# Expert stage of a fused attention and mixture-of-experts kernel: weight splits, PSUM banks, count loads and tile order rearranged

## The chip, the core and the metric

The kernel runs on one core of a Trainium2 chip. Five queues work side by side, each in its own order: PE (the matrix engine; its weight loads are listed as PEld), ACT (scalar engine), DVE (vector engine), POOL (GpSimd) and SP (which here only issues DMAs). They wait for each other through semaphores. The metric is the device time of one execution in microseconds (us); the median of several executions counts. The profile shows one execution, and its span is the time from the first to the last instruction.

## The reference

Attention with a block mask, a dense feed-forward layer, then a layer of eight experts of which each token takes one. The change touches only the experts:

```python
def _moe2_ref(x, w_gate, w1, w2, capacity):     # x [1152, 512], w1 [8, 512, 1024], w2 [8, 1024, 512]
    logits = x @ w_gate
    expert_idx = np.argmax(logits, axis=1)
    ...
    disp = np.zeros((E, capacity, D))           # capacity 288: slots of an expert
    ...                                         # token i goes to the next free slot of its expert
    h = np.maximum(np.einsum('ecd,edf->ecf', disp, w1), 0.0)
    y = np.einsum('ecf,efd->ecd', h, w2)
    ...
    out[i] = gate_w[i] * y[expert_idx[i], pos[i]]
```

## The kernel before

There are three parts: attention, the dense layer with the router at its end, and `part3`, the experts. Part 3 takes the time from about 330 us to the end. In it the order of every engine is the order in which the code is written.

Every fp32 product is made of three matmuls on a high and a low half of each operand: high by high, and the two mixed ones. So each weight tile must be split before it is used: ACT writes the high half (`xh`, line 1128), DVE the rest (`xl`, line 87). An expert has eight weight tiles of 512 KB, four of `w1` (raw tile `ra`) and four of `w2` (`rb`), loaded by SP into a ring of 12 raw buffers (`load_x`). While expert e is computed, the tiles of expert e+1 are split: the list `todo` holds a pair of functions for each tile (high, low), and `compute` runs a few of them between its own steps (`run(his, n)`, `run(los, n)`).

An expert has up to 288 slots, in tiles of 128, 128 and 32 slots (`j` = 0, 1, 2). A tile is computed only if the expert's count says that it holds tokens: each is an arm of a `tc.If` on a register. In the trace twelve tiles are computed: two for expert 0, one each for 1, 2 and 3, two for 4, three for 5, two for 6, none for 7. For a tile, `compute(e, j)` does on PE: two halves of `hx` (12 matmuls each, line 1207, ReLU into `hr` on ACT, line 1213), four transposes each (`hT`, line 1218) whose result ACT and DVE split into `gh` and `gl`, and 24 matmuls into `acc` (line 1228). ACT scales `acc` into `o` (line 1254) and POOL scatters `o` to the output (line 1255).

The slots of the next expert are loaded as `rows` (line 1169) and transposed on PE by `turn_slots` (`dT`, line 1177), then split into `dh` (ACT, line 1180) and `dl` (DVE). For j = 0 this is done inside the first tile (`turn_next`), for j = 1 and 2 after the tile's arm. The slots of expert 0 are made differently: part 2 gathers them by matmuls into four PSUM banks (`bank`, line 790), and `first_out` splits these into `dh` and `dl` (ACT line 802, DVE lines 800 and 87).

The counts lie in SBUF (`state["count"]`, ready at 326.0 us). `count_of(e)` loads one number into a register of PE, ACT, DVE and POOL (line 1265) and adds a check of its bounds.

PSUM has eight banks. Part 2 holds them in the order l1 (2), acc (3), m (2), lg (1); the `bank` tiles are the two of l1 and two of acc. Part 3 takes the banks over in the order in which its pools are opened.

Of the kernel before, what the change touches and what calls it, by code (L numbers as in the profile page):

```python
# [9 lines left out]
FP32 = mybir.dt.float32  # L10
# [7 lines left out]
PSUM = bass.MemoryType.PSUM  # L18
# [24 lines left out]
def attention_ffn_moe(  # L43
# [13 lines left out]
    nc = tc.nc  # L57
    B, H, S, D = q.shape
    NT, DM = out.shape
# [26 lines left out]
    def split_lo(eng, lo, x, hi):  # L86
        eng.tensor_tensor(out=lo, in0=x, in1=hi.bitcast(FP32), op=ALU.subtract)  # L87
# [4 lines left out]
    def load_w(pool, e, i):  # L92

        c = i // 2
        shape, src = [([128, 1, FE], w1[e, c * 128:(c + 1) * 128, :]), ([128, 2, DM], w2[e, c * 256:(c + 1) * 256, :])][i % 2]
        r = pool.tile(shape, FP32, tag="raw", name="r" + "ab"[i % 2])
        nc.sync.dma_start(out=r, in_=src.rearrange("(k p) f -> p k f", p=128))
        return r
# [601 lines left out]
    CT = (cap + 127) // 128  # L700
# [6 lines left out]
    state = {}  # L707
# [415 lines left out]
    def conv_x(e, i, r, part=0, parts=1):  # L1123

        n = FE // parts
        hi, lo, r = (x.rearrange("p k f -> p (k f)")[:, n * part:n * (part + 1)] for x in (*xw[e, i], r))
        return (
            lambda: nc.scalar.activation(out=hi, in_=r, func=ACTF.Copy),  # L1128
            lambda: split_lo(nc.vector, lo, r, hi),
        )  # L1130

    def part3():
        y_stack.close()
        p3 = ExitStack()
# [3 lines left out]
        hp = p3.enter_context(tc.tile_pool(name="hp", bufs=2, side="right"))  # L1138


        ps_acc = p3.enter_context(tc.tile_pool(name="ps_acc3", bufs=1, space=PSUM))
        ps_l1 = [p3.enter_context(tc.tile_pool(name=f"ps_l1{i}3", bufs=2, space=PSUM)) for i in range(2)]
        ps_m = p3.enter_context(tc.tile_pool(name="ps_m3", bufs=1, space=PSUM))
        ps_t = p3.enter_context(tc.tile_pool(name="ps_t3", bufs=2, space=PSUM))
        stiles = [(128 * i, min(128, CP - 128 * i)) for i in range(CT)]
        dT = state["dT"]
        views = bass_types.dram_disjoint_views(out, E * CT)
        NF = FE // 128
        rows, gate, xraw = {}, {}, {}
        engines = [mybir.EngineType.PE, mybir.EngineType.Activation, mybir.EngineType.DVE, mybir.EngineType.Pool]  # L1150


        COME = [0, 1, 2, 3, 4, 6, 5, 7]
        LATE = 2

        def load_x(e, half):

            xs = xraw.setdefault(e, {})
            for z in range(NX // 2 * half, NX // 2 * (half + 1)):
                xs[COME[z]] = load_w(raw_p if ((e - 1) * NX + z) % 12 < 4 else raw_q, e, COME[z])  # L1160

        def new_gate(e):
            gate[e] = dp.tile([128, CT, 2], FP32, tag="gt", name="gt")

        def load_rows(e):

            r = rows[e] = dp.tile([128, CT, YW], FP32, tag="rows", name="rows", bufs=1)
            for j, (s0, n) in enumerate(stiles):
                nc.sync.dma_start(out=r[0:n, j, :], in_=disp[e * CP + s0:e * CP + s0 + n, :])
            new_gate(e)  # L1170
# [14 lines left out]
        def passes(x, w):  # L1185
            return [(x[0], w[0]), (x[0], w[1]), (x[1], w[0])]

        def compute(e, j, side=(), turn_next=lambda: None):


            s0, n = stiles[j]
            h, hr, g = {}, {}, {}
            his, los = ([x[y] for x in side] for y in range(2))
            acc = ps_acc.tile([128, DM], FP32, tag="acc", name="acc")

            def run(fs, k):
                for f in fs[:k]:
                    f()
                del fs[:k]

            def l1(c, half):

                if half == 0:
                    h[c] = ps_l1[j > 0].tile([128, 512], FP32, tag="l1", name="hx")
                todo = [(x, y, kk) for x, y in ((0, 0), (0, 1), (1, 0)) for kk in range(KD)]
                for i, (x, y, kk) in list(enumerate(todo))[6 * half:6 * half + 6]:
                    nc.tensor.matmul(  # L1207
                        out=h[c][0:n], lhsT=dT[j][x][:, kk], rhs=xw[e, 2 * kk][y][:, 0, c * 512:(c + 1) * 512],
                        start=(i == 0), stop=(i == len(todo) - 1),
                    )  # L1210
                if half == 1:
                    hr[c] = hp.tile([128, 512], FP32, tag="hr", name="hr", bufs=3)
                    nc.scalar.activation(out=hr[c][0:n], in_=h[c][0:n], func=ACTF.Relu)

            def turn(c):
                ps = ps_m.tile([128, 4, 128], FP32, tag="m", name="hT")
                for i in range(4):
                    nc.tensor.transpose(  # L1218
                        out=ps[:, i, 0:n], in_=hr[c][0:n, i * 128:(i + 1) * 128], identity=ident[0:n, 0:n]
                    )  # L1220
                g[c] = gh, gl = [hp.tile([128, 4, 128], F32R, tag="g" + x, name="g" + x) for x in "hl"]
                nc.scalar.activation(out=gh[:, :, 0:n], in_=ps[:, :, 0:n], func=ACTF.Copy)
                split_lo(nc.vector, gl[:, :, 0:n], ps[:, :, 0:n], gh[:, :, 0:n])

            def l2(c, half):
                for f in range(4 * c + 2 * half, 4 * c + 2 * half + 2):
                    for i, (x, y) in enumerate(passes(g[c], xw[e, f // 2 * 2 + 1])):
                        nc.tensor.matmul(  # L1228
                            out=acc[0:n], lhsT=x[:, f % 4, 0:n], rhs=y[:, f % 2, :],
                            start=(f == 0 and i == 0), stop=(f == NF - 1 and i == 2),  # L1230
                        )

            run(his, 3)
            run(los, 3)
            l1(0, 0)
            l1(0, 1)
            run(his, 1)
            l1(1, 0)
            turn(0)
            run(his, 1)  # L1240
            run(los, 2)
            l1(1, 1)
            l2(0, 0)
            run(his, 1)
            turn(1)
            run(los, 1)
            l2(0, 1)
            run(his, NX)
            turn_next()
            run(los, NX)  # L1250
            l2(1, 0)
            l2(1, 1)
            y = hp.tile([128, DM], FP32, tag="hr", name="o", bufs=3)
            nc.scalar.mul(y[0:n], acc[0:n], gate[e][0:n, j, 0:1])  # L1254
            nc.gpsimd.indirect_dma_start(  # L1255
                out=views[e * CT + j],
                out_offset=bass.IndirectOffsetOnAxis(ap=gate[e][0:n, j, 1:2].bitcast(I32), axis=0),
                in_=y[0:n],
                in_offset=None,
                bounds_check=NT - 1,  # L1260
                oob_is_err=False,
            )

        def count_of(e):
            return nc.values_load(state["count"][0:1, e:e + 1], engines=engines, min_val=0, max_val=cap)  # L1265

        load_x(1, 0)
        load_x(1, 1)
        new_gate(0)
        for j, (s0, n) in enumerate(stiles):  # L1270
            nc.sync.dma_start(out=gate[0][0:n, j], in_=disp[s0:s0 + n, DM:DM + 2])
        count = {0: count_of(0)}
        for e in range(E):
            new = e + 1 < E
            todo = []
            if new:
                load_rows(e + 1)
                for i in COME:
                    new_x(e + 1, i, xraw[e + 1][i])
                todo = [conv_x(e + 1, i, xraw[e + 1][i]) for i in COME]  # L1280
            if e + 2 < E:
                load_x(e + 2, 0)

            def turn_next():
                if new:
                    turn_slots(e + 1, 0)

            with tc.If(count[e] > 0) as some:
                compute(e, 0, todo[:-LATE], turn_next)
            if new:  # L1290
                with some.Else():
                    for f in todo[:-LATE]:
                        f[0]()
                        f[1]()
                    turn_next()
            for f in todo[-LATE:]:
                f[0]()
                f[1]()
            if e + 2 < E:
                load_x(e + 2, 1)  # L1300
            for j in range(1, CT):
                with tc.If(count[e] > 128 * j):  # L1302
                    compute(e, j)
                if new:
                    turn_slots(e + 1, j)
            if new:
                count[e + 1] = count_of(e + 1)
        p3.close()

    every = {  # L1310
# [7 lines left out]
    with tc.manual_schedule(engines=every):  # L1318
        part3()
# [27 lines left out]
```

## Time and profile before

| what | value |
|---|---|
| median of 3 executions | 507.99 us (506.66 to 511.79) |
| profiled execution | 506.51 us, span 504.7 us |
| PE busy over the span | 479.9 us (95%) |
| DVE, ACT, POOL busy | 344.2, 311.9, 118.9 us |
| from first `hx` matmul to last `acc` matmul | 332.02 to 497.02 us |
| PE busy between 332 and 497 us | 157.29 us of 165 |

The busy time of PE counts matmuls that overlap in its pipeline, so a new matmul of 512 columns starts every 0.23 us though each is shown as 0.4 us. In a row of the timeline a bracket at the end tells how long the engine had been idle before it and what ended the wait; the inference of the releaser can name an engine that was long done.

### The profile page before, as it was taken

Reading aid. Unit: us, or ns where it says so; the run is one execution under the profiler, and the core shown is the slowest. Engines: PE = TensorE matmul, PEld = TensorE weight load, DVE = VectorE, ACT = ScalarE, POOL = GpSimd, SP = SyncE. Lnnn points to the kernel's source line nnn. Section 1 sums busy time; section 2 is a strip of 40 time slices with the busy share of each in tenths; the row PEclk is TensorE's granted clock in tenths of the full one; section 3 lists DMA queues with packets and bytes.
Section 4 is the critical chain, followed back from the end, with each engine's and each line's share of the span. In section 5 each row is a group of like instructions: output and inputs, shape, how many; then the busy total and the mean of one; then the engine's idle time right before and its main releaser. Section 6 shows DMA issues by size and latency. Waiting matters only on the chain. (4 is left out here: it accounts for less than half of the span.)

```text
span 504.7 us, 8722 instructions
## 1 busy us (share of the span) xinstructions
PE 479.9 (95%) x2842; PEld 400.2 (79%) x2842; DVE 344.2 (68%) x834; ACT 311.9 (62%) x701; POOL 118.9 (24%) x219
## 2 busy tenths in 40 slices
PE   6899999999999999999999999989998989999994
PEld 6778887789998899999998988768776768786683
DVE  6789898869987999964554466565467974551451
ACT  4789899957775765643554455365567784652641
POOL 6477878530000000000000102501122330101211
PEclk9999999999999999999999999789999999999998
DMA  8788674314998873520130034278379876370100
GB/s 194 162 224 213 156 191 103 114 44 126 234 238 280 259 235 111 166 85 0 56 112 2 22 125 147 89 272 318 111 299 358 310 283 246 114 290 21 54 22 24
DMA packets 61254, 80.86 MB, mean 160 GB/s; under 512 B 33170, under 2 KB 33170, under 8 KB 61200
## 3 DMA queue, kind: packets, MB, share of 16 engines
q1 hardware_dynamic: 58368, 75.18, 48.6%
q0 software_dynamic: 1632, 4.72, 2.5%
q8 instruction: 28, 0.46, 0.4%
q10 hardware_dynamic: 1200, 0.30, 0.3%
q14 instruction: 26, 0.21, 0.1%
HBM read 62.17 MB, written 12.41 MB: 148 GB/s over the span
## 5 line engine op out<-in xcount | busy, mean ns | idle before, releaser
L260 PE MATMUL acc<-wbh,gh 128*128 128x512 f32 x144 | 57.3, 398 | 0.0
L260 PE MATMUL acc<-wbh,gl 128*128 128x512 f32 x144 | 57.1, 397 | 0.0
L260 PE MATMUL acc<-wbl,gh 128*128 128x512 f32 x144 | 57.1, 397 | 0.0
L916 POOL DMA_INDIRECT disp<-y_all,slot x9 | 9.1, 1014 | 199.9 <-DVE e L245 177.2
L87 DVE TENSOR_TENSOR xl<-rb,xh 128x1024 fp32r<-128x1024 f32 (+1 forms) x36 | 38.9, 1101 | 22.2 <-ACT xh L1128 22.2
L485 POOL TENSOR_SCALAR prob<-prob,stat 128x576 f32<-128x576 f32 (+3 forms) x80 | 42.0, 537 | 26.6 <-DVE stat L479 17.9
L458 ACT ACTIVATE prob<-s,stat 128x288 f32<-128x288 f32 (+4 forms) x96 | 45.3, 480 | 1.5 <-POOL kk L339 0.8
L243 ACT ACTIVATE e<-h 128x384 f32<-128x384 f32 x48 | 23.2, 484 | 36.7 <-PE h L233 34.3
L186 DVE SCALAR_TENSOR_TENSOR cv_t<-r,cv_t 128x512 int32<-128x512 int32 x64 | 44.2, 691 | 0.3
L87 DVE TENSOR_TENSOR xl<-ra,xh 128x1024 fp32r<-128x1024 f32 (+1 forms) x36 | 39.3, 1102 | 7.0 <-ACT xh L1128 6.1
L233 PE MATMUL h<-xh,wah 128*128 128x384 f32 x192 | 42.2, 341 | 0.2 <-DVE e L245 0.2
L233 PE MATMUL h<-xl,wah 128*128 128x384 f32 x192 | 41.6, 337 | 0.0
L233 PE MATMUL h<-xh,wal 128*128 128x384 f32 x192 | 41.1, 336 | 0.0
L245 DVE SCALAR_TENSOR_TENSOR e<-e,h 128x384 f32<-128x384 f32 x48 | 26.4, 550 | 21.3 <-ACT e L244 21.1
L1228 PE MATMUL acc<-xh,gh 128*128 128x512 f32 (+1 forms) x96 | 39.3, 410 | 0.0
L445 DVE TENSOR_REDUCE stat<-s 128x1 f32<-128x288 f32 (+4 forms) x96 | 37.5, 422 | 1.4 <-PE s L423 1.1
L233 PEld LDWEIGHTS h<-xh,wah 128*128 128x128 f32 x192 | 34.3, 188 | 4.9 <-DVE e L245 0.9
L1228 PE MATMUL acc<-xh,gl 128*128 128x512 f32 (+1 forms) x96 | 38.0, 395 | 0.0
L1228 PE MATMUL acc<-xl,gh 128*128 128x512 f32 (+1 forms) x96 | 37.8, 394 | 0.0
L1255 POOL DMA_INDIRECT out<-o,gt x12 | 11.7, 972 | 110.7 <-ACTq L1302 33.1
L1128 ACT ACTIVATE xh<-ra 128x1024 fp32r<-128x1024 f32 (+1 forms) x36 | 34.3, 962 | 5.0 <-PE h L233 2.8
L249 ACT ACTIVATE gh<-e 128x384 fp32r<-128x384 f32 x48 | 25.1, 523 | 16.6 <-DVE e L245 16.0
(172 smaller groups left out, 1174.8 us busy)
## 6 DMA issues: line engine op xcount, KB each, us to landing
ra<-in_moe_w SPq DMA_DIRECT2D x32, 512.0 KB, 5.9
rb<-in_moe_w SPq DMA_DIRECT2D x32, 512.0 KB, 7.4
r<-in_moe_w_in SPq DMA_DIRECT2D x16, 512.0 KB, 6.8
r<-in_moe_w_out SPq DMA_DIRECT2D x16, 512.0 KB, 4.0
disp<-z SPq DMA_DIRECT2D x18, 257.0 KB, 7.0
rows<-disp SPq DMA_DIRECT2D x14, 257.0 KB, 4.9
out<-z SPq DMA_DIRECT2D x9, 256.0 KB, 3.9
kr<-in_k SPq DMA_DIRECT2D x16, 128.0 KB, 3.3
```

Source lines behind the costliest of these rows:

```text
L87: eng.tensor_tensor(out=lo, in0=x, in1=hi.bitcast(FP32), op=ALU.subtract)
L186: nc.vector.scalar_tensor_tensor(out=st["t"], in0=x(), scalar=scalar, in1=st["t"], op0=op, op1=ALU.bitwise_or)
L233: nc.tensor.matmul(out=h[:, f, :], lhsT=w[:, kk, (f0 + f) * 128:(f0 + f + 1) * 128], rhs=x[:, kk, t0:t0 + n], start=(i == 0), stop=(i == l ...
L243: nc.scalar.activation(out=e, in_=hf, func=ACTF.Relu, scale=-1.0)
L245: nc.vector.scalar_tensor_tensor(out=e, in0=e, scalar=-1.0, in1=hf, op0=ALU.add, op1=ALU.max)
L249: nc.scalar.activation(out=gh, in_=ef, func=ACTF.Copy)
L260: nc.tensor.matmul(out=acc[t], lhsT=x[:, f, t * 128:(t + 1) * 128], rhs=w[:, f0 + f, :], start=(first and f == 0 and i == 0), stop=(last a ...
L445: nc.vector.tensor_reduce(out=stat[n][0][0:nq, t + b:t + b + 1], in_=banks[n, part, b][0:nq, c0:c0 + w], axis=AX.X, op=ALU.max, negate=True,)
L458: nc.scalar.activation(out=prob[n, part][0:nq, c0 + k0:c0 + k0 + w], in_=banks[n, part, b][0:nq, c0:c0 + w], func=ACTF.Exp, bias=stat[n][0 ...
L485: nc.gpsimd.tensor_scalar(out=p, in0=p, scalar1=stat[n][2][0:nq, t:t + 1], scalar2=0.0, op0=ALU.mult, op1=ALU.add)
L1128: lambda: nc.scalar.activation(out=hi, in_=r, func=ACTF.Copy),
L1228: nc.tensor.matmul(out=acc[0:n], lhsT=x[:, f % 4, 0:n], rhs=y[:, f % 2, :], start=(f == 0 and i == 0), stop=(f == NF - 1 and i == 2),)
```

## The change

1. **Splits.** The first arm gets all eight high splits, and the low splits but the last two; before, the last two tiles (`LATE`) were split after the arm, high and low. Inside `compute`, two tiles instead of three are split before the first `hx`, and most of the rest after `turn_next`, that is behind `gh` and `dh`.
2. **PSUM.** The pools of part 3 are opened in another order, so that the first `hx` lies where part 2 had its pool m.
3. **Counts.** All eight counts are loaded by one instruction on each engine, ahead of the first expert, and the check of the bounds is gone.
4. **Order.** The arms of j = 1 and 2 follow each other; both `turn_slots` come after them.
5. **Buffers.** `hr` gets one buffer and `o` two of its own; before, they shared three.
6. **Loads.** The `rows` of expert 1 are asked for ahead of the second half of its weights.

```diff
+        ps_l1 = [None, p3.enter_context(tc.tile_pool(name="ps_l113", bufs=2, space=PSUM))]
+        ps_t = p3.enter_context(tc.tile_pool(name="ps_t3", bufs=2, space=PSUM))
+        ps_m = p3.enter_context(tc.tile_pool(name="ps_m3", bufs=1, space=PSUM))
+        ps_l1[0] = p3.enter_context(tc.tile_pool(name="ps_l103", bufs=2, space=PSUM))
         ps_acc = p3.enter_context(tc.tile_pool(name="ps_acc3", bufs=1, space=PSUM))
-        ps_l1 = [p3.enter_context(tc.tile_pool(name=f"ps_l1{i}3", bufs=2, space=PSUM)) for i in range(2)]
-        ps_m = p3.enter_context(tc.tile_pool(name="ps_m3", bufs=1, space=PSUM))
-        ps_t = p3.enter_context(tc.tile_pool(name="ps_t3", bufs=2, space=PSUM))
...
-                    hr[c] = hp.tile([128, 512], FP32, tag="hr", name="hr", bufs=3)
+                    hr[c] = hp.tile([128, 512], FP32, tag="hr", name="hr", bufs=1)
...
-            run(his, 3)
-            run(los, 3)
+            run(his, 2)
+            run(los, 2)
             l1(0, 0)
             l1(0, 1)
-            run(his, 1)
             l1(1, 0)
             turn(0)
             run(his, 1)
-            run(los, 2)
+            run(los, 1)
             l1(1, 1)
             l2(0, 0)
             run(his, 1)
             turn(1)
             run(los, 1)
             l2(0, 1)
+            turn_next()
             run(his, NX)
-            turn_next()
             run(los, NX)
...
-            y = hp.tile([128, DM], FP32, tag="hr", name="o", bufs=3)
+            y = hp.tile([128, DM], FP32, tag="o", name="o")
...
-        def count_of(e):
-            return nc.values_load(state["count"][0:1, e:e + 1], engines=engines, min_val=0, max_val=cap)
-
         load_x(1, 0)
+        load_rows(1)
         load_x(1, 1)
...
-        count = {0: count_of(0)}
+        _, count = nc.values_load_multi_w_load_instructions(
+            state["count"], engines=engines, min_val=0, max_val=cap,
+            skip_runtime_bounds_check_because="a sum of ones, and its minimum with cap",
+        )
...
-                todo = [conv_x(e + 1, i, xraw[e + 1][i]) for i in COME]
+                his, los = zip(*(conv_x(e + 1, i, xraw[e + 1][i]) for i in COME))
...
-                compute(e, 0, todo[:-LATE], turn_next)
+                compute(e, 0, (his, los[:-LATE]), turn_next)
...
-            for f in todo[-LATE:]:
-                f[0]()
-                f[1]()
+            for f in los[-LATE:]:
+                f()
...
-                if new:
+            if new:
+                for j in range(1, CT):
                     turn_slots(e + 1, j)
-            if new:
-                count[e + 1] = count_of(e + 1)
```

On PE, at the entrance to the experts: the last matmul of part 2, the load of the count, the branch, and the first `hx` of expert 0, with the queues that each waits for. Before:

```order
L790 MATMUL bank<-one,xl 128x288
L1265 TENSOR_LOAD count [waits DVE_49,Activation_49,Pool_49]
L1265 ISA x2
L1288 COMPARE_AND_BRANCH
L1207 MATMUL hx<-xh,dh_2041 128x512 [waits DVE_49,PE_49,Activation_49]
L1207 MATMUL hx<-xh,dh_2041 128x512 x3
L1207 MATMUL hx<-xl,dh_2041 128x512 x4
L1207 MATMUL hx<-xh,dl_2042 128x512 x4
```

And now:

```order
L790 MATMUL bank<-one,xl 128x288
L1271 TENSOR_LOAD count [waits DVE_49,Activation_49,Pool_49]
L1292 COMPARE_AND_BRANCH
L1209 MATMUL hx<-xh,dh_2041 128x512 [waits DVE_49,PE_49]
L1209 MATMUL hx<-xh,dh_2041 128x512 [waits Activation_49] x3
L1209 MATMUL hx<-xl,dh_2041 128x512 x4
L1209 MATMUL hx<-xh,dl_2042 128x512 [waits DVE_49]
```

The two instructions that check the bounds are gone, and one wait ahead of the first `hx` has become waits of single matmuls on the slices of `dh` and `dl` that they read.

On ACT, the first arm of an expert, from the branch at its head to `o`. Before:

```order
L1128 ACTIVATE xh<-ra 128x1024
L1128 ACTIVATE xh<-rb 128x1024
L1128 ACTIVATE xh<-ra 128x1024
L1213 ACTIVATE hr<-hx 128x512
L1128 ACTIVATE xh<-rb 128x1024
L1222 ACTIVATE gh<-hT 128x512
L1128 ACTIVATE xh<-ra 128x1024
L1213 ACTIVATE hr<-hx 128x512
L1128 ACTIVATE xh<-ra 128x1024
L1222 ACTIVATE gh<-hT 128x512
L1180 ACTIVATE dh_2041<-dT 128x512
L1254 ACTIVATE o<-acc,gt 128x512
```

And now:

```order
L1128 ACTIVATE xh<-ra 128x1024
L1128 ACTIVATE xh<-rb 128x1024
L1215 ACTIVATE hr<-hx 128x512
L1224 ACTIVATE gh<-hT 128x512
L1128 ACTIVATE xh<-ra 128x1024
L1215 ACTIVATE hr<-hx 128x512
L1128 ACTIVATE xh<-rb 128x1024
L1224 ACTIVATE gh<-hT 128x512
L1182 ACTIVATE dh_2041<-dT 128x512
L1128 ACTIVATE xh<-ra 128x1024 x2
L1128 ACTIVATE xh<-rb 128x1024 x2
L1255 ACTIVATE o<-acc,gt 128x512
```

Two `xh` instead of three stand ahead of the first `hr`, four stand between `dh` and `o` where none stood, and the two that followed the arm are among these.

On PE, the end of an expert: the end of the arm of j = 2, the transposes of the next expert's slots, and the branch into the next expert. Before:

```order
L1302 UNCONDITIONAL_BRANCH x2
L1177 MATMUL dT<-ident,rows 128x32 x4
L1265 TENSOR_LOAD count
L1265 ISA x2
L1288 COMPARE_AND_BRANCH
L1207 MATMUL hx<-xh,dh_2041 128x512 x4
```

And now:

```order
L1304 UNCONDITIONAL_BRANCH x2
L1179 MATMUL dT<-ident,rows 128x128 x4
L1179 MATMUL dT<-ident,rows 128x32 x4
L1292 COMPARE_AND_BRANCH
L1209 MATMUL hx<-xh,dh_2041 128x512 x4
```

The transposes for j = 1 have come down from between the two arms, and the load of the next count has gone from between the transposes and the branch.

## Rows read from the trace of the kernel before

**Rows 1.** Waits of PE from 300 to 505 us: total, times, longest.

```profile
PE hT L1218 <- ACT hr L1213: 2.9, 3, 1.1
PE dT L1177 <- PEq L1302: 2.7, 9, 0.3
PE hx L1207 <- DVE dl L87: 2.3, 1, 2.3
PE hx L1207 <- ACT xh L1128: 1.3, 3, 0.4
...
PE hx L1207 <- ACTq L1302: 0.5, 1, 0.5
```

**Rows 2.** Timeline of PE at the entrance: start, duration, line, idle before.

```profile
329.41 0.32 PE L790 MATMUL bank<-one,xl 128*128 128x288 f32 x1
332.02 1.34 PE L1207 MATMUL hx<-xh,dh 128*128 128x512 f32 x4 [2.29 <-DVE dl L87]
...
337.84 0.60 PE L1218 MATMUL hT<-ident,hr 128*128 128x128 f32 x4
```

**Rows 3.** Windows: length, PE, PEld, DVE, ACT, POOL busy; granted clock; DMA share, GB/s.

```profile
329.00:330.00 1.00, 0.73 (x4) 0.50 (x3) 0.64 (x3) 0.72 (x4) 0.00 (x0) 0.78 0.04 12
...
332.00:333.00 1.00, 0.98 (x4) 0.87 (x5) 0.00 (x0) 0.89 (x1) 0.00 (x0) 0.93 0.69 254
333.00:334.00 1.00, 1.00 (x3) 0.73 (x3) 0.74 (x1) 1.00 (x2) 0.00 (x0) 0.50 1.04 426
```

**Rows 4.** Timeline of ACT at the entrance.

```profile
329.41 1.58 ACT L802 ACTIVATE dh<-bank 128x128 fp32r<-128x128 f32 x6 [0.20 <-PE bank L790]
...
332.11 1.06 ACT L1128 ACTIVATE xh<-ra 128x1024 fp32r<-128x1024 f32 x1 [0.53 <-DVE dl L87]
```

**Rows 5.** Line 1265, the count: ns min/median/max, first and last start.

```profile
L1265 PEldq TENSOR_LOAD <-count x8: 297/302/492, 326.1 to 497.8; - x8
L1265 PEldq FUSED_REGOPS  x8: 146/146/160, 326.7 to 498.2; - x8
...
L1265 ACTq TENSOR_LOAD <-count x8: 274/278/477, 331.5 to 498.5; - x8
```

**Rows 6.** Timeline of PE, expert 1 and the start of expert 2.

```profile
360.02 1.19 PE L1207 MATMUL hx<-xh,dh 128*128 128x512 f32 x4 [0.52 <-ACT dh L1180]
...
364.29 0.60 PE L1218 MATMUL hT<-ident,hr 128*128 128x128 f32 x4
...
373.03 0.63 PE L1177 MATMUL dT<-ident,rows 128*128 128x128 f32 x4 [0.30 <-PEq L1302]
...
374.80 1.19 PE L1207 MATMUL hx<-xh,dh 128*128 128x512 f32 x4 [0.43 <-ACT xh L1128]
...
380.29 0.66 PE L1218 MATMUL hT<-ident,hr 128*128 128x128 f32 x4 [1.04 <-ACT hr L1213]
```

**Rows 7.** Timeline of ACT, same stretch.

```profile
369.98 0.60 ACT L1180 ACTIVATE dh<-dT 128x512 fp32r<-128x512 f32 x1 [1.23 <-PE dT L1177]
372.82 0.69 ACT L1254 ACTIVATE o<-acc,gt 128x512 f32<-128x512 f32 x1 [2.24 <-PEq L1302]
373.40 1.99 ACT L1128 ACTIVATE xh<-rb 128x1024 fp32r<-128x1024 f32 x2
...
376.79 1.07 ACT L1128 ACTIVATE xh<-ra 128x1024 fp32r<-128x1024 f32 x1 [0.17 <-issue]
...
379.65 0.58 ACT L1213 ACTIVATE hr<-hx 128x512 f32<-128x512 f32 x1
```

**Rows 8.** Line 1302 from 498.7 to 500 us: branches past empty expert 7.

```profile
L1302 PEldq COMPARE_BRANCH  x2: 218/322/427, 498.9 to 499.6; - x2
```

**Rows 9.** Timelines of SP's DMA issues and of POOL after the entrance.

```profile
333.93 1.88 SPq L1169 DMA_DIRECT2D rows<-disp  x3
...
341.01 1.09 POOL L1182 COPY gt<-rows 128x1 f32<-128x1 f32 x1 [13.21 <-DMA rows<-disp]
```

**Rows 10.** Window over expert 3, columns as in Rows 3.

```profile
390.87:406.96 16.09, 13.99 (x68) 10.70 (x68) 12.24 (x14) 11.93 (x17) 4.70 (x8) 1.00 0.91 328
```

More of the change, by code (lines that the diff above doesn't have):

```diff
@@ L1186, in passes, with compute @@
             return [(x[0], w[0]), (x[0], w[1]), (x[1], w[0])]
-        def compute(e, j, side=(), turn_next=lambda: None):
+        def compute(e, j, side=((), ()), turn_next=lambda: None):
             s0, n = stiles[j]
             h, hr, g = {}, {}, {}
-            his, los = ([x[y] for x in side] for y in range(2))
+            his, los = (list(x) for x in side)
             acc = ps_acc.tile([128, DM], FP32, tag="acc", name="acc")
@@ L1271, in part3 @@
             nc.sync.dma_start(out=gate[0][0:n, j], in_=disp[s0:s0 + n, DM:DM + 2])
-        count = {0: count_of(0)}
+        _, count = nc.values_load_multi_w_load_instructions(
+            state["count"], engines=engines, min_val=0, max_val=cap,
+            skip_runtime_bounds_check_because="a sum of ones, and its minimum with cap",
+        )
         for e in range(E):
             new = e + 1 < E
-            todo = []
+            his = los = []
             if new:
-                load_rows(e + 1)
+                if e:
+                    load_rows(e + 1)
                 for i in COME:
                     new_x(e + 1, i, xraw[e + 1][i])
-                todo = [conv_x(e + 1, i, xraw[e + 1][i]) for i in COME]
+                his, los = zip(*(conv_x(e + 1, i, xraw[e + 1][i]) for i in COME))
             if e + 2 < E:
@@ L1288, in part3 @@
             with tc.If(count[e] > 0) as some:
-                compute(e, 0, todo[:-LATE], turn_next)
+                compute(e, 0, (his, los[:-LATE]), turn_next)
             if new:
                 with some.Else():
-                    for f in todo[:-LATE]:
-                        f[0]()
-                        f[1]()
+                    for f in (*his, *los[:-LATE]):
+                        f()
                     turn_next()
-            for f in todo[-LATE:]:
-                f[0]()
-                f[1]()
+            for f in los[-LATE:]:
+                f()
             if e + 2 < E:
```

## The prediction, made before the changed kernel was run

> **What bounds the kernel now.** I read the chain of work that ended last first. As far back as it reaches, through three experts, it is matmuls of PE up to the last `acc`, so the experts end when PE has done its work, and all the change can win is PE time lost. That time stands in the view of PE's waits [rows 1], which has three kinds. One wait of 2.3 us at the entrance. Nine of 0.3 us ahead of `dT`, and five of 0.4 to 0.5 ahead of `hx`, all between experts (the fifth, 0.52, stands in rows 6). Three that sum to 2.9 us ahead of `hT`, where PE wants `hr` and ACT has not written it. Together 10.2 us. A fourth loss is no wait: in a window after the entrance PE's granted clock is 0.50, that is 1.2 GHz, though PE is busy [rows 3]; over an expert later it is 1.00 [rows 10].
>
> The timelines then tell what is late. At the entrance PE goes idle at 329.73 (329.41 + 0.32) and starts `hx` at 332.02 [rows 2], just after the last split of the gathered slots: the first `hx` lies in a bank that those splits still read. Between experts, rows 6 show the gap of 0.30 after a branch past an arm and of 0.43 ahead of `hx`; the load of the count takes PE 0.30 us and a step of its bounds check 0.15 [rows 5], which is that gap. In expert 2, `hT` waits 1.04 us: ACT writes `hr` at 379.65 because two late `xh` (373.40) and then three more (from 376.79) stand ahead of it [rows 7].
>
> **The change part by part.** Sums are made against the profiled execution, 506.5 us.
>
> *Entrance: banks, rows and one load.* The first `hx` now needs the slices of `dh` of the first 128 slots only. They are two of ACT's six from 329.41 at 0.26 each [rows 4], so ready by 329.95, and `hx` needs the last as its fourth matmul, 0.7 us after 329.73: PE should go on without the gap of 2.29 us. Before, it went from `hx` to `hT` in 5.82 us (332.02 to 337.84 [rows 2]); in expert 1 at full clock the same 18 matmuls took 4.27 (360.02 to 364.29 [rows 6]). The missing 1.55 us are the low clock. The clock was back at 1.00 from about 329.4 (0.78 in that window) and fell at about 332.9 (0.93) [rows 3], 0.9 us into the work that followed the idle stretch; idle stretches of 1.04 us and less later left it at 1.00 [rows 6, 10], so without the gap I take it to stay up, and PE wants `hT` at 329.73 + 4.27 = 334.0. Now ACT is late. Its first `xh` started at 332.11 [rows 4]; one `xh` takes 0.95 (three from 376.79 to 379.65 [rows 7]), so `hr` starts at 334.0 after two, ends at 334.6, and `hT` starts at 334.7: 3.1 us earlier than 337.84.
>
> Between ACT's splits and that `xh` stands the load of the counts, now eight numbers. On PE it is issued at 326.1, far ahead; on ACT at 331.5, where it took up to 0.48 for one number [rows 5]. The trace has no load of several. Low end: no longer than for one. High end: eight times 0.28, 2.24 us, or 1.8 more. I take the middle between the ends, some 0.7 more than now, since no row is nearer to either. The Trainium skill (Runtime: NRT & Kernel Launch, section Instruction fetch mechanics) has a rule against the change here: a register load costs some 200 ns for each register even in bulk. By it eight numbers would cost an estimated 1.4 us more than one; by the row of one number they could cost nothing more. So `hT` starts 2.4 us earlier; bounds 0 (the bank still waits) and 3.1.
>
> The rows of expert 1 move ahead of four weight loads on SP. They were issued from 333.93, behind those and three small loads of the gates, and reached POOL at 341.01 [rows 9]. PE would want them for `dT` 5 us after `hT`, at 340.4: unmoved they would cost 0.6, moved nothing. The four weight loads go some 2 us later (1.88 for the issue of the rows); ACT wants them only behind `dh`, at about 341, where a delay reaches only `o`. If they came later still, the tile of j = 1 would cover some 12 us.
>
> *The load of the count between experts.* At expert 0 to 1 and 4 to 5, `hx` waited 0.52 and some 0.5 us [rows 1, 6]. Without load and check, and with 0.9 us of transposes ahead of the branch, PE's sequencer should be ahead again: 2 x 0.5 = 1.0 us won (bounds 0.8 and 1.0).
>
> *Tiles back to back.* After experts 1, 2 and 3 both further tiles are empty. Before: 0.30 + 0.30 + 0.43 = 1.03 us idle [rows 6]. Now the two skips follow each other with nothing between to cover the second. Low price: none beyond the first gap of 0.30, since the gap of 0.30 after the first arm already contains two branches in a row (past the other arm and past j = 1). High price: 0.7, the spacing of such branches on PE where nothing covers them [rows 8]. I take 0.4, halfway: 0.33 won each, 1.0 in all (bounds 0.1 and 2.2). The same page and section of the skill state that a taken branch out of the fetched window forces a fetch of its target. By that the price is that of rows 8 and this term 0.1 instead of 1.0; the gaps of 0.30 give it no support, since they do not grow with a second branch.
>
> *Splits in the first arm.* In experts 2, 3 and 4, `hx` to `hT` takes 5.49 us (374.80 to 380.29) against 4.27 in expert 1 [rows 6], so each wait costs 1.22, and the three 3.7. Afterwards, on ACT, counted from a tile's first `hx`: `dh` starts at +9.96 (369.98 - 360.02); then `dh` 0.48, four `xh` 3.8, `o` 0.58 (372.82 to 373.40 [rows 7]), two skipped arms 0.5, two `dh` 0.75, a branch 0.17, two `xh` 1.9: `hr` starts at +18.1 and ends at +18.7. On PE: `acc` ends at +12.7 (373.03 - 0.30), 0.7 of skips, 0.9 of transposes, so the next `hx` starts at +14.3 and `hT` is wanted at +18.5. A wait of 0.2 to 0.3 stays, with the restart 0.5 us: 0.7 won each, 2.1 in all. The bounds are 0 (ACT falls 0.5 us behind this count) and 3.7 (the wait vanishes). What else is late: `o` ends 2 us after `acc`, but the bank is wanted 6 us into the next tile; DVE's last two `xl` end 3 us after the arm, and the halves they write are read 10 us later. SP's third and fourth load of the next weights wait for `xl` that now stand behind `gl`, up to 3 us later; their data are wanted some 14 us after that.
>
> *Buffers.* One `hr` is enough, since PE transposes the first before it finishes the second `hx`; `o` waits for a scatter two tiles old. Both cost nothing and win nothing.
>
> Sum: 2.4 + 1.0 + 1.0 + 2.1 = 6.5 us; 506.5 - 6.5 = **500.0 us**. The median of the three runs is 1.5 us above the profiled execution, so on it the same sum gives 501.5; I stay with the profiled one, as the lowest of the three agrees with it to 0.2.
>
> **The rivals.**
>
> 1. *The load of eight numbers holds ACT.* By rows 5, eight times one number. Then `hr` ends 1.1 us later than I take, `hT` waits 2.6 us, longer than the gap that preceded the low clock, and 1.55 us more are lost: 6.5 - 1.1 - 1.5 = 3.9 won, 502.6. The page named above speaks for it; against it, that one instruction fetches neighbouring words.
> 2. *ACT stays late.* If the skips of two arms cost it 0.5 us more, or a DMA share of 0.91 over 16.1 us [rows 10], which the shorter expert of some 15 us pushes to 0.98, delays the raw tiles, the `hT` waits stay: 2.1 less, 502.1.
> 3. *More than forecast.* The skips overlap, the load costs nothing more and `hr` is in time: 3.1 + 1.0 + 2.2 + 3.7 = 10.0, 496.5.
> 4. *The change does not do what it says at the bank:* another reader of the new bank keeps the 2.29 us; 2.4 less, 502.4. Against it, the new program waits slice by slice.
> 5. *Slower: the low clock stays.* At 0.50 a microsecond does 0.54 of the work (4.27 of 18 matmuls at full clock; 0.43 against 0.23 for one). If the clock, at 0.50 while the slots are gathered, is raised by nothing when work goes on without a gap, then every us of it costs 0.46, and it decides from 6.5 / 0.46 = 14 us on. Through the whole first tile, 12.7 us of work take 23.5: +10.8, so 510.8. Against it: in the trace it rose at about 329.4, before the gap had begun [rows 3].
>
> **How the numbers follow.** Chances: forecast 0.50, rival 1 0.15, rival 2 0.15, rival 3 0.10, rival 4 0.05, rival 5 0.05. A measurement of this kernel can tell about 1%, 5 us, from no change. The forecast and rival 3 win more than 5 us, with 0.07 of the forecast's own spread below that and a few of the rivals' above: faster 0.60. Rivals 1, 2 and 4 win 3.9 to 4.4, within 1%: 0.34. Slower 0.06. The range reaches from near rival 3 to past rivals 1, 2 and 4 counted on the median: 497 to 505.
>
> **What would show it.** Right: the first `hx` within 0.5 us of the last gather matmul and the clock at 1.00 from there; `hT` of expert 0 near 335.4; no gap ahead of `hx`; one gap of 0.5 to 0.9 us after experts 1 to 3; `hT` waits of 0.5 us or less in experts 2 to 4; ACT's load in the profile tells the price of eight numbers. Wrong: raw tiles that ACT waits for behind `dh`, a low clock in the first tile, or skips that cost PE more than 1 us.

## The result and the profile after

The changed kernel took a median of 501.13 us (four executions, 500.62 to 505.69) against 508.61 us for the kernel before (four, 506.66 to 511.79): a ratio of 0.988, 95% interval 0.985 to 0.992, so 1.2% faster. The profiled execution is one of the four: 501.24 us, span 499.5 us, 5.3 us less than the profiled execution of before.

Two things that the change does not touch differ between the two profiled executions and must be taken out first. The gathering of the slots begins at 326.35 us after and at 323.48 before, so the first two parts, whose code is the same, were 2.87 us later. And the gather itself, 24 matmuls into `bank`, takes 5.93 us before and 4.81 after from its first to its last start, because PE's clock is at 1.2 GHz for a longer or shorter part of it. In the fourteen profiled kernels of this study the gather took 3.3 us in six, 4.7 to 4.8 in seven and 5.9 in one. So I measure a **stage**: from the start of the last gather matmul to the end of the last `acc`. It is 167.6 us before and 160.7 after: 6.9 us won, of which the time shows 5.3 (6.9 + 1.1 for the gather - 2.9 for the late start = 5.1, and 0.2 elsewhere). The medians differ by 7.5 us; only one execution of each kernel was profiled, so how the rest divides is not shown.

Waits of PE from 330 to 505 us in the changed kernel, the view of [rows 1] (total, times, longest). The wait of 2.3 us at the entrance is gone. The skips cost as much as before (2.9 against 2.7 us), one wait ahead of `hT` is left, at another place, and the waits ahead of `hx` have ACT's queue as their releaser:

```profile
PE dT L1179 <- PEq L1304: 2.9, 5, 0.8
PE hx L1209 <- ACTq L1304: 1.5, 3, 0.5
PE hT L1220 <- ACT hr L1215: 1.1, 1, 1.1
```

Together 5.5 us, against 10.2. At the entrance, the timeline of PE after (start, duration, line, idle before), which answers to [rows 2]:

```profile
331.16 0.29 PE L790 MATMUL bank<-one,xl 128*128 128x288 f32 x1
331.29 1.09 PE L1209 MATMUL hx<-xh,dh 128*128 128x512 f32 x4
...
336.72 0.66 PE L1220 MATMUL hT<-ident,hr 128*128 128x128 f32 x4 [1.08 <-ACT hr L1215]
```

The gap of 2.29 us is gone, and the first `hT` starts 5.56 us after the last gather matmul, where it was 8.43. The windows of after (columns as in [rows 3]) show the clock at 0.50 in the gather and back at 1.00 from 331 us on:

```profile
329.00:330.00 1.00, 1.00 (x6) 1.00 (x6) 0.00 (x0) 0.00 (x0) 0.69 (x2) 0.50 0.41 156
...
331.00:332.00 1.00, 1.00 (x8) 0.85 (x7) 0.73 (x4) 0.94 (x5) 0.00 (x0) 1.00 0.69 263
333.00:334.00 1.00, 1.00 (x6) 0.82 (x5) 0.66 (x6) 0.37 (x2) 0.00 (x0) 1.00 0.00 0
```

ACT is the late one now, as its timeline says (compare [rows 4]): splits of the slots to 333.37, then the load of the counts, then two `xh`, then `hr`:

```profile
332.98 0.39 ACT L802 ACTIVATE dh<-bank 128x32 fp32r<-128x32 f32 x2 [0.20 <-DVE dl L87]
334.18 1.06 ACT L1128 ACTIVATE xh<-ra 128x1024 fp32r<-128x1024 f32 x1 [0.81 <-DVE dl L87]
335.15 1.04 ACT L1128 ACTIVATE xh<-rb 128x1024 fp32r<-128x1024 f32 x1
336.09 0.58 ACT L1215 ACTIVATE hr<-hx 128x512 f32<-128x512 f32 x1
```

The 0.81 us ahead of the first `xh` are the load of eight numbers, whose rows are these (min/median/max in ns; compare [rows 5]):

```profile
L1271 PEldq TENSOR_LOAD <-count x1: 1048/1048/1048, 328.6 to 328.6; - x1
...
L1271 ACTq TENSOR_LOAD <-count x1: 757/757/757, 333.3 to 333.3; - x1
```

At the border from expert 1 to 2, PE after (compare [rows 6]):

```profile
371.83 0.99 PE L1179 MATMUL dT<-ident,rows 128*128 128x128 f32 x8 [0.73 <-PEq L1304]
373.36 1.20 PE L1209 MATMUL hx<-xh,dh 128*128 128x512 f32 x4 [0.54 <-ACTq L1304]
```

and ACT in the same stretch (compare [rows 7]):

```profile
368.35 0.60 ACT L1182 ACTIVATE dh<-dT 128x512 fp32r<-128x512 f32 x1 [1.23 <-PE dT L1179]
368.85 2.00 ACT L1128 ACTIVATE xh<-ra 128x1024 fp32r<-128x1024 f32 x2
370.74 1.99 ACT L1128 ACTIVATE xh<-rb 128x1024 fp32r<-128x1024 f32 x2
372.63 0.68 ACT L1255 ACTIVATE o<-acc,gt 128x512 f32<-128x512 f32 x1
373.74 0.77 ACT L1182 ACTIVATE dh<-dT 128x512 fp32r<-128x512 f32 x2 [0.43 <-ACTq L1304]
```

Read the two together. Two skipped arms in a row cost PE 0.73 us at once. Then a wait that was not there: PE is through with the transposes at 372.8, but ACT, behind four `xh`, ends `o` at 373.31, and PE starts `hx` 0.05 us later; its releaser is ACT's queue at the end of the arms. The border costs 1.27 us where it cost 1.03. In return `hT` no longer waits in experts 2, 3 and 4, and the start of expert 3 follows that of expert 2 by 15.02 us instead of 16.08.

### The profile page after: what moved, and what is told of

The parts are those of the page before. It is cut to its first block, busy times and chain, and to the rows that moved or that the text cites. A ratio compares the mean times of both kernels' runs of the same rounds, so it can differ in the third digit from the quotient of the medians.

```text
span 499.5 us, 8666 instructions
## 1 busy us (share of the span) xinstructions
PE 477.7 (96%) x2842; PEld 398.5 (80%) x2842; DVE 344.1 (69%) x834; ACT 311.3 (62%) x701; POOL 119.3 (24%) x219
## 5 line engine op out<-in xcount | busy, mean ns | idle before, releaser
L87 DVE TENSOR_TENSOR gl<-hT,gh 128x512 fp32r<-128x512 f32 (+1 forms) x24 | 15.8, 658 | 43.1 <-ACT gh L1224 43.1
L1256 POOL DMA_INDIRECT out<-o,gt x12 | 13.9, 1160 | 107.5 <-ACT o L1255 45.1
```

The lines of the kernel that those rows point to most:

```text
L1256: nc.gpsimd.indirect_dma_start(out=views[e * CT + j], out_offset=bass.IndirectOffsetOnAxis(ap=gate[e][0:n, j, 1:2].bitcast(I32), axis=0), ...
```

## The experiments

The table gives, in us, from the timeline of PE of each profiled execution: the first `hT` of expert 0 after the start of the last gather matmul; the time from tile to tile of expert 0 (two tiles) and of experts 2 and 3; the stage; and the time. There is one execution of each, so I read nothing from a difference of stages below 0.3 us. Two things that are not in an edit can stand in a stage:

- Six of the stages hold one stretch of some 3 us at a clock of 0.50: before, counts_only and order_only at the entrance, splits_only in the second tile of expert 0, rows_late and between in expert 3. It costs some 1.5 us (in before 5.82 us from `hx` to `hT`, where banks_old takes 4.27). The other eight hold none. Without it the stage of before would be some 166.0 us, and the change would win 5.4.
- A stage is counted from the last gather matmul, but SP issues the rows and weights of expert 1 at a time that goes with the first one: the rows 7.1 us after it in after, whose gather takes 4.8 us, and 7.3 in both_between, whose gather takes 3.3. Behind a short gather PE and ACT can come too early for them.

| kernel | first hT | expert 0 | expert 2 | expert 3 | stage | time |
|---|---|---|---|---|---|---|
| before | 8.43 | 14.12 + 13.88 | 16.08 | 16.09 | 167.6 | 506.51 |
| after | 5.56 | 13.78 + 13.29 | 15.02 | 15.03 | 160.7 | 501.24 |
| banks_only | 6.16 | 15.54 + 15.60 | 16.00 | 16.16 | 168.3 | 507.26 |
| counts_only | 8.29 | 14.52 + 14.85 | 15.78 | 15.77 | 168.6 | 504.95 |
| splits_only | 6.84 | 13.27 + 17.68 | 15.02 | 14.99 | 167.5 | 506.03 |
| order_only | 8.40 | 14.12 + 14.97 | 15.89 | 15.76 | 168.2 | 507.69 |
| banks_old | 6.92 | 12.59 + 13.29 | 15.03 | 15.00 | 162.0 | 501.26 |
| rows_late | 5.56 | 16.18 + 13.27 | 15.03 | 16.56 | 164.6 | 503.04 |
| counts_old | 5.23 | 13.44 + 13.36 | 15.03 | 15.00 | 160.8 | 498.95 |
| between | 5.50 | 13.70 + 13.29 | 15.02 | 16.59 | 162.0 | 502.36 |
| one_more | 5.56 | 13.76 + 13.29 | 14.50 | 14.38 | 159.0 | 498.36 |
| entrance | 4.32 | 12.47 + 13.95 | 15.01 | 15.01 | 160.1 | 501.04 |
| both | 4.31 | 12.50 + 13.29 | 14.52 | 14.39 | 157.7 | 497.24 (median of 5; profiled 498.68) |
| both_between | 4.34 | 12.51 + 14.02 | 14.33 | 14.30 | 157.9 | 494.99 |

### One part alone, on the kernel before

**banks_only**: the pools of part 3 in the new order, nothing else.

```diff
-        ps_acc = ...; ps_l1 = [...]; ps_m = ...; ps_t = ...
+        ps_l1 = [None, ...]; ps_t = ...; ps_m = ...; ps_l1[0] = ...; ps_acc = ...
```

> The kernel before with the new order of PSUM pools alone. The stage is counted from the start of the last gather matmul to the end of the last acc matmul: 167.6 us before, 160.7 after the whole change. My theory: the bank alone made the gap of 2.29 us and with it the low clock; PE goes on without a gap at clock 1.00, and hT of expert 0 then waits for an hr that stands behind three xh on ACT: hT some 6.2 us after the start of the last gather matmul instead of 8.4, the stage 165.4 us. Rival: the gap is not the cause of the low clock, or ACT's three xh hold hT as long as the gap did: the stage 167 us or more.

The gap ahead of `hx` vanished, the clock stayed up and the first `hT` came 2.3 us earlier, as my theory had it, but the stage is 0.7 us longer than before. The timeline of PE shows where it went, three new waits inside expert 0:

```profile
335.67 0.66 PE L1219 MATMUL hT<-ident,hr 128*128 128x128 f32 x4 [1.67 <-ACT hr L1214]
...
341.90 0.66 PE L1178 MATMUL dT<-ident,rows 128*128 128x128 f32 x4 [0.94 <-DMA rows<-disp]
...
354.36 0.66 PE L1219 MATMUL hT<-ident,hr 128*128 128x128 f32 x4 [1.58 <-ACT hr L1214]
```

ACT still has three `xh` ahead of `hr`, the rows still stand behind the weights, and the third wait belongs to a step that I had priced at nothing (below). The rival's number came, but not by what it named: two of the three waits stand in neither theory. Alone the banks win nothing.

**counts_only**: eight counts at once, no bounds check, no load between experts.

```diff
-        count = {0: count_of(0)}
+        _, count = nc.values_load_multi_w_load_instructions(state["count"], ...)
...
-                count[e + 1] = count_of(e + 1)
```

> The kernel before with one load of all counts alone, no check. My theory: the gaps of 0.4 to 0.5 us ahead of hx at five borders between experts are the load and its check, and go: 2.3 us less, the stage 165.3 us. Rival: PE waits there for ACT, as the wait view names ACT; the gaps stay, and the stage is 167.6 us.

All five gaps of 0.4 to 0.5 us ahead of `hx` vanished. But in experts 2 to 4 ACT was late anyway, and `hT` now waits 1.25 us each instead of 1.0, so the period falls by 0.3 of the 0.43 won at the border. What the other borders won is lost to a new wait of PE for `hr` in the second tile of expert 0 (1.36 us) and another in expert 5 (0.85). The first of these `hr`, on ACT:

```profile
352.39 0.60 ACT L1213 ACTIVATE hr<-hx 128x512 f32<-128x512 f32 x1 [2.82 <-DMA out<-o,gt]
```

`hr` waits for the scatter of the first tile's `o` to land. In the kernel before, `hr` and `o` share three buffers, and ACT's instructions before name the semaphores of the scatters ahead of the second `hr` of a tile; in the changed kernel they do not. In `before` itself ACT waited here too, 0.93 us, without making PE wait:

```profile
352.55 0.60 ACT L1213 ACTIVATE hr<-hx 128x512 f32<-128x512 f32 x1 [0.93 <-DMA out<-o,gt]
```

In all four kernels of one part this wait is 2.8 to 3.6 us and makes PE wait 1.36 to 2.09; in the changed kernel and all that are built on it, each of which has own buffers, it occurs nowhere.

**splits_only**: the new lists of splits and their places in `compute`, as in the diff.

```diff
-            run(his, 3)
-            run(los, 3)
+            run(his, 2)
+            run(los, 2)
...
-                    for f in todo[:-LATE]:
+                    for f in (*his, *los[:-LATE]):
```

> The kernel before with the new places of the splits alone. My theory: the three hT waits go (3.7 us), but the first hx of an expert now waits until ACT has ended the first arm of the expert before, whose o stands behind four xh; that is some 15.0 us after the start of that expert's first hx, where the load of the count let PE start at 14.8: 0.2 us lost three times, the stage 164.5 us, and hx gaps of 0.6 to 0.7. Rival: PE does not wait for ACT there; the hx gaps stay at 0.43 and the stage is 163.9 us or less.

The periods of experts 2 and 3 are 15.02 and 14.99, those of the whole change. The `hT` waits are gone and a wait for ACT's end of the arm has come, so neither the counts nor the order is needed for this. The rest was lost in one tile; PE there:

```profile
354.65 0.97 PE L1218 MATMUL hT<-ident,hr 128*128 128x128 f32 x4 [2.09 <-ACT hr L1213]
...
377.62 1.20 PE L1207 MATMUL hx<-xh,dh 128*128 128x512 f32 x4 [0.57 <-ACTq L1299]
```

The 2.09 us are the wait for the scatter again. The clock fell behind it, 0.71 from 354 to 356 us and 0.50 from 356 to 358, and the tile took 17.68 us against 13.29 in the changed kernel.

**order_only**: both transposes of the next slots behind the arms of j = 1 and 2.

```diff
             for j in range(1, CT):
                 with tc.If(count[e] > 128 * j):
                     compute(e, j)
-                if new:
-                    turn_slots(e + 1, j)
+            if new:
+                for j in range(1, CT):
+                    turn_slots(e + 1, j)
```

> The kernel before with both turn_slots behind the arms alone. My theory: two skips in a row cost PE 0.30 and 0.45, more than 0.30 and 0.30 apart, and the load's gap of 0.43 stays: 0.15 us more three times, the stage 168.0 us. Rival, as in the prediction: eight transposes in a row cover the load, so the gap ahead of hx goes: 1 us less or more, the stage 166.6 us or less.

The two skips cost 0.72 to 0.83 us at once, where two single ones cost 0.30 each, but no gap stands ahead of `hx` any more:

```profile
390.98 0.99 PE L1177 MATMUL dT<-ident,rows 128*128 128x128 f32 x8 [0.83 <-PEq L1302]
391.98 1.19 PE L1207 MATMUL hx<-xh,dh 128*128 128x512 f32 x4
```

So the rival was right on the gap, and the periods fall by 0.2 to 0.3 us instead of rising. The stage is 0.6 us longer than before, near the 168.0 of my theory, but by luck: the second tile of expert 0 pays the scatter (1.41).

### One part taken out of the changed kernel

**banks_old**: the pools in the order of before.

```diff
-        ps_l1 = [None, ...]; ps_t = ...; ps_m = ...; ps_l1[0] = ...; ps_acc = ...
+        ps_acc = ...; ps_l1 = [...]; ps_m = ...; ps_t = ...
```

> The changed kernel with the old order of PSUM pools. My theory: the gap of some 2.3 us ahead of the first hx comes back, and with it some 3.4 us of half clock; since hr then waits for nothing that hx does not, the 1.08 us ahead of hT go: 2.7 us lost, the stage 163.4 us. Rival: the other entrance edits (rows first, two xh) made the gain, and the stage stays within 1 us of 160.7.

It lies between the two: 162.0, so the banks are worth 1.3 us here and not 2.7. The gap came back, and here it was longer than before:

```profile
332.42 1.17 PE L1208 MATMUL hx<-xh,dh 128*128 128x512 f32 x4 [2.36 <-DVE dl L87]
```

But the clock did not fall behind it: the windows give 1.00 from 328 to 338 us. From `hx` to `hT` it took 4.27 us, so the gap cost its own length less the 1.08 us that PE waits for `hr` in the changed kernel: 2.36 - 1.08 = 1.28.

**rows_late**: the rows of expert 1 asked for behind all its weights.

```diff
-        load_rows(1)
         load_x(1, 1)
...
-                if e:
-                    load_rows(e + 1)
+                load_rows(e + 1)
```

> The changed kernel with the slots of expert 1 asked for behind all its weights, as before. By the prediction the transposes in the first tile of expert 0 then wait 0.6 us for them (0.9 if the wait is as long as with the banks alone): that tile takes 14.4 to 14.7 us instead of 13.78. Rival: the weights of expert 1, now earlier, let ACT finish earlier, and the second tile gives it back: both tiles together stay at 27.1.

The wait came, and it was over three times the size:

```profile
342.36 0.66 PE L1179 MATMUL dT<-ident,rows 128*128 128x128 f32 x4 [2.19 <-DMA rows<-disp]
```

The first tile took 2.4 us more, and the second gave nothing back. Some of this is the short gather of 3.3 us: PE wanted the rows 14.2 us after the first gather matmul and had them after 16.35. In after PE wants them after 15.5 us (341.85), so behind its gather the wait would be an estimated 0.8 us. The rest of the longer stage is a low clock in expert 3 (0.50 from 390 to 392 us), whose period is 16.56.

**counts_old**: one count loaded for each expert, with its check, behind the transposes.

```diff
-        _, count = nc.values_load_multi_w_load_instructions(state["count"], ...)
+        count = {0: count_of(0)}
...
             if new:
                 for j in range(1, CT):
                     turn_slots(e + 1, j)
+                count[e + 1] = count_of(e + 1)
```

> The changed kernel with one count loaded per expert, as before. By my theory PE waits at borders 1 to 2, 2 to 3 and 3 to 4 for ACT's end of the arm anyway (0.5 us), and a load lies beside that: periods 15.0 to 15.1 there; only at borders 0 to 1 and 4 to 5 a gap of 0.4 to 0.5 returns, and ACT's shorter load at the entrance gives 0.3 back: the experts end 166.1 us after the first gather matmul against 165.5. Rival: every border pays 0.43, periods 15.45, end 167.4.

The borders pay almost nothing: periods of 15.03, and 13.36 and 13.53 us where the changed kernel has 13.29 and 13.44. So the transposes ahead of the branch cover the load, also at the two borders where I expected a gap of 0.4 to 0.5. At the entrance `hT` is 0.33 us earlier, since ACT loads one number and not eight. The stage is the same within 0.2: loading all counts at once wins nothing in this order. Its lower time goes with a gather of 3.3 us, 1.5 less than after's, that also began 0.95 us earlier.

**between**: the transposes back between the arms.

```diff
-            if new:
-                for j in range(1, CT):
-                    turn_slots(e + 1, j)
+                if new:
+                    turn_slots(e + 1, j)
```

> The changed kernel with turn_slots back between the arms. My theory: the second skip again costs 0.30 instead of 0.45, but PE waits for ACT's end of the arm anyway, so the sum of the gaps at a border of two skips stays at 1.3 us, and the stage 160.7 us within 0.3. Rival: the back-to-back skips are what makes PE late, and the stage is 160.0 us or less.

Where the clock stayed up, the period is 15.01, as expected, since PE waits for ACT's end of the arms in either order. Expert 3 took 16.59, with the same waits ahead of it; the windows show why:

```profile
389.00:390.00 1.00, 1.00 (x4) 0.81 (x3) 0.85 (x2) 1.00 (x2) 1.00 (x1) 0.50 1.15 426
390.00:391.00 1.00, 1.00 (x4) 0.71 (x4) 0.85 (x3) 1.00 (x2) 1.00 (x5) 0.50 0.97 346
391.00:392.00 1.00, 1.00 (x4) 0.81 (x3) 1.00 (x2) 0.14 (x1) 0.71 (x1) 0.50 1.02 375
```

Without these 1.6 us its stage would be some 160.5, as long as after's. Tiles back to back win nothing.

### What is late now, taken away

**one_more**: one of the four `xh` behind `dh` goes to an earlier place in the arm, where ACT waits for PE.

```diff
             run(his, 1)
             turn(1)
+            run(his, 1)
             run(los, 1)
```

> The changed kernel with one more xh ahead of turn_next, in the 1.2 us in which ACT waits for dT. My theory: three instead of four xh stand ahead of o, ACT ends the first arm 0.95 us earlier, and the gaps of 0.46 to 0.54 us ahead of the first hx of experts 2, 3 and 4 go: the stage 159.2 us against 160.7. Rival: these gaps come from the branches or the register on PE, not from ACT; they stay, and the stage is 160.7 us.

The wait for ACT's end of the arms is gone; this is all that PE waits for from 330 us on:

```profile
PE dT L1179 <- PEq L1305: 2.1, 4, 0.8
PE hT L1220 <- ACT hr L1215: 1.0, 1, 1.0
PE dT L1179 <- DVE xl L87: 0.8, 1, 0.8
```

The stage is 1.7 us shorter, and the wait was indeed ACT's `o`, not the branches.

**entrance**: no split ahead of the first `hx` of expert 0.

```diff
-            run(his, 2)
-            run(los, 2)
+            run(his, 2 if e else 0)
+            run(los, 2 if e else 0)
```

> The changed kernel without xh ahead of the first hr in expert 0. My theory: hT of expert 0 waits 1.08 us only for the two xh that stand ahead of hr on ACT; without them the wait goes, and the work moved behind is covered by the second tile: the stage 159.5 us. Rival: the splits are then late for expert 1 (ACT behind in its first tile, a wait ahead of the hx of expert 1 or its hT): no gain, 160.7 us or more.

The first `hT` is 1.24 us earlier and no longer waits; half of that comes back in the second tile, 0.44 us of it ahead of an `hT`. The stage is 0.6 shorter, halfway between the theory and its rival.

**both**: the two edits together.

> Both improvements together: one high split more in the middle of the arm, and no splits ahead of the first product of expert 0. If ACT's end of the arm and ACT's first two splits were the two places that bounded the changed kernel, the gains add: the experts end 161.7 us after the first gather matmul (162.3 with the one, less 0.6), or 163.2 if the clock is low for a part of the gather; the time is near 498, 0.978 of the kernel before, and experts 1 to 3 keep periods of 14.5. Rival: the 0.6 us come back as a longer wait in the second tile of expert 0, where the splits now stand; then it is as with the one alone, 162.3 and 498.4.

The gains add, and more: 157.7, which is 3.0 us shorter than after, since the wait of `entrance` in the second tile does not occur with the `xh` moved forward. PE waits for no `hr` any more:

```profile
PE dT L1179 <- PEq L1305: 2.0, 4, 0.7
PE dT L1179 <- DVE xl L87: 0.8, 1, 0.8
```

The median of five executions is 497.24 us (495.85 to 498.68), a ratio to the kernel before of 0.976, interval 0.974 to 0.978. The changed kernel's own interval, against the kernel before on another occasion, begins at 0.985, so this version is faster than both.

**both_between**: this version with the order of before.

> The improved kernel with the tile order of before (transposes between the arms). With ACT no longer late, this shows what the order alone is worth. By the prediction tiles back to back win 0.33 us at each of three borders, so the periods of experts 1 to 3 go from 14.5 to 14.8. Rival, from the gaps seen: two skips in a row cost 0.8 at once, two single ones 0.30 and 0.36, so the old order is 0.1 to 0.2 better and the periods are 14.3 to 14.5.

The rival holds. PE has two gaps of 0.30 us at a border instead of one of 0.8:

```profile
367.36 0.63 PE L1179 MATMUL dT<-ident,rows 128*128 128x128 f32 x4 [0.30 <-PEq L1305]
368.29 0.40 PE L1179 MATMUL dT<-ident,rows 32*128 32x32 f32 x4 [0.30 <-PEq L1305]
```

and periods of 14.30 to 14.33. The second tile of expert 0 takes 0.7 us more, 0.51 of it a wait ahead of an `hT`, so the stages are alike. But that wait is hardly the order's. ACT waits 0.62 us for weights at the end of the first tile, so `o` and the `hr` behind it come that much later:

```profile
341.57 1.07 ACT L1128 ACTIVATE xh<-rb 128x1024 fp32r<-128x1024 f32 x1 [0.27 <-DMA rb<-in_moe_w]
342.99 1.06 ACT L1128 ACTIVATE xh<-rb 128x1024 fp32r<-128x1024 f32 x1 [0.35 <-DMA rb<-in_moe_w]
```

In `both`, whose gather is 1.5 us longer, ACT waits for no weights there. That leaves some 0.2 us to the order in this tile. The time, the lowest of all, is one execution in which the gather took 3.3 us and began 2.0 us earlier than in after; whether this version is faster than `both` stays open.

## Why the prediction was right

The sum was right (6.5 us forecast, 6.9 measured over the stage; 500.0 against a median of 501.13). Two terms came near their size. The other two missed in opposite directions, because the prediction had wrong where ACT makes PE wait, and that they cancel is luck. So is a part of the size: some 1.5 of the 6.9 us are the low clock in the one execution of before that was profiled, and it came with the gap in three of five kernels only.

- **Entrance, forecast 2.4 us: 2.9.** The gap vanished, `hx` followed within 0.13 us, the clock stayed up, and ACT became the late one, as the prediction said. Its two halves are told apart by `banks_old`: 1.3 us are the gap, net of the wait for ACT; the rest is the low clock. That the gap brings the low clock was too strong: from `hx` to `hT` PE worked 5.6 to 5.8 us at the lower clock in three of the five kernels with the gap (before, counts_only, order_only) and 4.3 at full clock in two (splits_only, banks_old). In the nine without the gap it never fell there.
- **Load of eight numbers, taken as 0.7 more: 0.28 more** on ACT (757 ns against 477 for the first load of before). Rival 1 falls. This trace has (757 - 278) / 7 = 68 ns for each further number on ACT and (1048 - 302) / 7 = 107 on PE. The Trainium skill (Runtime: NRT & Kernel Launch, section Instruction fetch mechanics) has some 200 ns for each register even in bulk; the trace does not agree, and the measurement decides.
- **Rows moved, taken as 0.6 avoided: 2.2** by `rows_late`, an estimated 0.8 behind a gather as long as after's. The mechanism was right. In `rows_late` PE asked for them 14.2 us after the first gather matmul, where my figure of 340.4 is 16.9: I counted from an execution whose gather was 2.6 us slower.
- **Count load between experts, forecast 1.0 us.** At the two borders after a second tile the time fell by 0.59 and 0.40, which is the sum, but not by the load of all counts at once: `counts_old` pays less than 0.1 there. Either edit alone removes the gap (`counts_only`, `order_only`); together they win it once.
- **Tiles back to back, forecast 1.0 us won: nothing** (`between` has the same periods where its clock stayed up). The price of the second skip was right (0.4 forecast; 0.73 to 0.83 us for both against 0.30 for one). What the step missed is ACT. I had counted `o` ending 2 us after `acc` and said only the bank depends on it; PE's branch into the next expert waits for ACT's end of the arms as well, 0.46 to 0.54 us three times. So each border went from 1.03 to about 1.27 us, and of the three signs for the borders one failed: a gap ahead of `hx` is there.
- **Splits in the first arm, forecast 2.1 us: about 3.0.** The `hT` waits vanished, worth 3.7, and the waits at the borders, which `splits_only` has with the old order too, take 0.7 back. `splits_only` has the same periods without the order and the counts, so the 3.0 us, forecast as 3.1 for this term and the one before it, are the splits' alone. The count of ACT was right: counted from the first `hx` of expert 1 (358.36), `hr` of expert 2 starts at +18.16, where the forecast has +18.1, right behind the second `xh`:

```profile
375.34 1.06 ACT L1128 ACTIVATE xh<-rb 128x1024 fp32r<-128x1024 f32 x1
376.52 0.60 ACT L1215 ACTIVATE hr<-hx 128x512 f32<-128x512 f32 x1
```

  What the step missed is PE's start: it is held at the border and begins `hx` at +15.0 instead of +14.3, so that it wants `hT` only when ACT has `hr`. `one_more`, where the border has no such wait and `hT` has none either, shows what it costs: 0.5 to 0.7 us in each period.
- **Buffers, taken as nothing:** a step that failed. Before, the second `hr` of a tile waits for a scatter to land. Against the kernel before that wins nothing, since PE did not wait there yet. But it is a condition of the other gains: in all four kernels of one part the second tile of expert 0 lost 1.4 to 2.1 us to it. Neither the buffers alone nor the changed kernel without them was run; the wait is shown by the traces of kernels with and without them.

Rivals 2 and 4 did not come about: no `hT` wait in experts 2 to 4, no wait at the bank. Rival 3 came true in the `hT` waits alone: the skips did not overlap, and `hr` of expert 0 was 1.1 us late. Rival 5 did not come about either: the clock rose in the gather, with no idle stretch.

## What to carry to other kernels

When several engines are near their limit, an edit that wins a gap for one hands the wait to the next: here none of the four parts that were run alone shortened the stage by more than 0.1 us, and the whole change won 6.9. So look, for each gap that is to go, which instruction PE wants next and what stands ahead of it, down to buffers that two tiles share with a scatter. And the end of a conditional arm is a meeting point: the last instruction of a slower engine in it can hold the next arm of all of them, so work that is moved "off the path" belongs in the middle of an arm, where that engine waits anyway.

## What was not expected of the hardware

The clock is not the same from execution to execution of the same code. Ahead of the gather PE has the same idle stretches of 0.51 and 0.40 us in all fourteen traces. The clock fell to 1.2 GHz (granted 0.50) at 322.6 us, inside the first of them, in before, and at 326.8, behind both, in after; it stayed at 2.4 in one_more and banks_old. That is a difference of 1.5 to 2.6 us before any changed instruction. The border from expert 2 to 3 costs about 1.3 us idle in after, between and rows_late alike; it was followed by some 3 us at 0.50 in the latter two and by none in after. A wait of 2.19 us in rows_late left the clock at 1.00, and one of 2.09 in splits_only did not. So none of these idle stretches by itself tells whether the clock falls. Each fall in a stage costs some 1.5 us, which is a fifth of what the whole change wins.
